# One load of a streamed key cache cut into six, a ring of buffers at another address, and sixteen idle matmuls

## The chip, the cores and the metric

The kernel runs on one core of one Trainium2 chip. Its time is the device time of one execution in microseconds; the kernel before takes 1294.54 us (median of three runs, 1294.46 to 1294.87). Five engines work beside each other: TensorE (PE, its weight loads shown as PEld), VectorE (DVE), ScalarE (ACT), GpSimd (POOL) and SyncE (SP), which here only issues DMAs. The DMAs of the core run on 16 DMA engines; a queue is the way from one issuing engine to those 16.

## The reference

One decoding step of a transformer layer: grouped-query attention over a cache, plus a token-mixing MLP, both on the same normalised input. All arrays are float32.

```python
x: (8, 1, 512); k_cache, v_cache: (8, 8, 8192, 128)      # 268 MB each
q = (layernorm(x) @ wq)                                  # 32 heads of 128, 4 to a cache head
p = softmax(q @ k^T * 128**-0.5)                         # 8192 keys per head
out = x + (p @ v) @ wo + W2 gelu(W1 layernorm(xn) + b1) + b2
```

Each cache element is read once and used by four query heads. The two caches are 536.9 MB of the 553.7 MB that the kernel reads.

## The kernel before, in words

The work runs in 32 steps (`N_PR`). Step `i` takes one batch element and two cache heads: 2 x 8192 keys of 128 numbers, 8 MB of keys and 8 MB of values, laid over 128 partitions with 64 KB in each. One load of a step, keys or values, is a single DMA of 128 rows of 64 KB (`load_next`, L109), issued by SP. The first and last steps use halves of 4 MB (L111).

All loads land in one ring of five slots, `raw`, each of 32 KB in a partition (`slots`, L48). Keys of neighbouring steps lie in slots 0 and 1 or 1 and 2, in turn; values lie in slots 3 and 4. So one slot of the keys of step `i+1` is one that keys of step `i` used, and their load is issued when the first half of the keys of step `i` is scored. The ring stands behind a small tile, `pad` (L46), which holds three weight columns of the MLP and a one-hot table: 74 float32 in a partition, 296 bytes. In the built program, the ring starts at byte 16832 of a partition.

Order is written by hand: `manual_schedule` keeps each engine's instructions as they are coded. In a step, for each half of the keys, DVE turns four blocks in place (L251, four transposes of 2.27 us), and TensorE scores each block (L261); then the row maximum, the exponential, the spread of the probabilities, and TensorE's product with the values of the step before (L302). SP issues the next keys after the first half (`score_half`) and the next values after the product. In the last step the two halves of `wo` follow in the same ring, the second half cut into pieces of 8, 4, 2, 1 and 1 sixteenths of it (L123), so that the closing matmuls (L432, L438) begin before all is there. The output leaves by one DMA of 4 x 8 rows of 512 bytes (L446).

At the start x and b2 are loaded by ACT's queue, the columns for `pad` by POOL's, and `wq` and the first keys by SP's. DVE builds tables (`ident` comes from POOL; `rep`, `hmask`, `send` and others from DVE), TensorE projects the queries (L221, L232) when `wq` is there.

## Time and profile before

| what | value |
|---|---|
| median of three runs | 1294.54 us (1294.46 to 1294.87) |
| the profiled execution: its time, and the span of its instructions | 1294.56 us, 1292.8 us |
| mean granted TensorE clock | 0.808 |
| busy share of the span: PE, DVE, ACT, POOL | 58%, 52%, 16%, 17% |
| DMA: bytes, mean rate | 554.39 MB, 429 GB/s |

The span runs from the first to the last instruction of the program; 1.76 us of the profiled execution's time lie outside it. Shares are means over the whole span. A DMA share of 1.00 in a window means that all 16 DMA engines had a packet under way all the time; a packet is counted in the window in which it starts, so that the share of a short window can be over 1.

### The profile page before, as it was taken

Reading aid. Unit: us, or ns where it says so; the run is one execution under the profiler, and the core shown is the slowest. Engines: PE = TensorE matmul, PEld = TensorE weight load, DVE = VectorE, ACT = ScalarE, POOL = GpSimd, SP = SyncE. Lnnn points to the kernel's source line nnn. Section 1 sums busy time; section 2 is a strip of 40 time slices with the busy share of each in tenths; the row PEclk is TensorE's granted clock in tenths of the full one; section 3 lists DMA queues with packets and bytes.
Section 4 is the critical chain, followed back from the end, with each engine's and each line's share of the span. In section 5 each row is a group of like instructions: output and inputs, shape, how many; then the busy total and the mean of one; then the engine's idle time right before and its main releaser. Section 6 shows DMA issues by size and latency. Waiting matters only on the chain.

```text
span 1292.8 us, 10743 instructions
## 1 busy us (share of the span) xinstructions
PE 751.4 (58%) x4630; PEld 162.6 (13%) x4630; DVE 677.8 (52%) x509; ACT 206.9 (16%) x311; POOL 225.9 (17%) x241
## 2 busy tenths in 40 slices
PE   4366456666556665465575656575455765455566
PEld 1011011111011111011110111111011110011112
DVE  3656654455644465654365644466644565544460
ACT  0002222121222121122111222112222000000000
POOL 0003323131332122233113322212332000000000
PEclk9688777887677897787987877887777887778888
DMA  9999999999999999999999999999999999999997
GB/s 407 428 433 447 424 432 435 432 436 426 439 432 430 430 432 436 432 431 435 430 443 422 435 434 424 443 426 430 442 424 439 430 434 430 428 441 423 434 426 313
DMA packets 11011, 554.39 MB, mean 429 GB/s; under 512 B 1324, under 2 KB 1356, under 8 KB 1748
## 3 DMA queue, kind: packets, MB, share of 16 engines
q1 hardware_dynamic: 10836, 553.67, 99.2%
q8 instruction: 36, 0.59, 0.2%
q14 instruction: 11, 0.09, 0.0%
q0 software_dynamic: 96, 0.02, 0.0%
q10 hardware_dynamic: 32, 0.02, 0.0%
HBM read 553.69 MB, written 0.02 MB: 428 GB/s over the span
## 4 chain that ended last, share of the span: by engine, by line
DMA 73%; DVE 22%; PE 4%; issue 0%; SPq 0%; DVEq 0%
DMA raw<-in_A_k_cache_dram 69%; DVE raw L251 22%; PE acc L261 3%; DMA raw<-in_A_wo_dram 3%; DMA raw<-in_A_wq_dram 2%; PE misc L221 0%; PE acc L302 0%; SPq L123 0%; DVEq L251 0%; PE hb L438 0%; SPq L80 0%; PE misc L279 0%; DVE macc L445 0%; DVEq L445 0%
## 5 line engine op out<-in xcount | busy, mean ns | idle before, releaser
L251 DVE STREAM_TRANSPOSE raw<-raw 128x2048 f32<-128x2048 f32 x256 | 565.4, 2274 | 250.4 <-DMA raw<-in_A_k_cache_dram 250.4
L261 PE MATMUL acc<-raw,z 128*32 128x512 f32 x2048 | 371.3, 810 | 486.9 <-DVE raw L251 474.3
L302 PE MATMUL acc<-raw,pt 128*32 128x512 f32 x2048 | 243.2, 617 | 16.1 <-DMA raw<-in_A_v_cache_dram 15.9
L348 POOL TENSOR_SCALAR g<-g,pad 128x512 f32<-128x512 f32 x112 | 77.4, 691 | 577.7 <-ACT g L347 577.7
L261 PEld LDWEIGHTS acc<-raw,z 128*32 128x32 f32 x2048 | 47.1, 123 | 798.4 <-DVE raw L251 492.8
L349 POOL TENSOR_TENSOR macc<-macc,g 128x512 f32<-128x512 f32 x112 | 141.8, 1266 | 9.3
L287 ACT ACTIVATE t2k<-acc,nb 128x512 f32<-128x512 f32 x32 | 22.0, 687 | 651.9 <-DVE nb L281 651.9
L294 DVE STREAM_TRANSPOSE pt<-misc 128x512 f32<-128x512 f32 x64 | 45.9, 717 | 141.0 <-PE misc L293 136.6
L347 ACT ACTIVATE g<-hb,pad 128x512 f32<-128x512 f32 x112 | 87.0, 777 | 192.4 <-POOL macc L349 191.0
L302 PEld LDWEIGHTS acc<-raw,pt 128*32 128x32 f32 x2048 | 67.2, 113 | 174.5 <-issue 138.7
L281 DVE CUSTOM_DVE_ANT_0 t2k<-misc,hmask 128x128 f32<-128x128 f32 x32 | 9.3, 292 | 121.5 <-PE misc L279 121.5
L293 PE MATMUL misc<-t2k,send 128*128 128x512 f32 x128 | 65.0, 631 | 2.7 <-ACT t2k L287 2.7
L274 DVE TENSOR_REDUCE mr<-acc 128x1 f32<-128x512 f32 x32 | 22.1, 691 | 46.1 <-PE acc L261 46.1
L310 ACT COPY ob<-acc 128x512 f32<-128x512 f32 x32 | 18.7, 585 | 121.6 <-PE misc L326 55.1
L341 POOL MEMSET macc<- 128x512 f32 x8 | 4.2, 526 | 185.0 <-PE misc L353 154.4
L347 ACT ACT_TABLE_LOAD x24 | 30.8, 1283 | 17.9 <-PE hb L339 17.6
L416 ACT ACT_TABLE_LOAD x24 | 30.8, 1283 | 0.4
L326 PE MATMUL misc<-ob,pick 128*32 128x512 f32 (+2 forms) x72 | 29.0, 545 | 0.7 <-ACT ob L310 0.7
L293 PEld LDWEIGHTS misc<-t2k,send 128*128 128x128 f32 x128 | 22.2, 193 | 44.7 <-issue 41.8
L221 PE MATMUL misc<-raw,ob 128*32 128x512 f32 x64 | 10.9, 843 | 12.3 <-DVE mv L145 8.4
L328 DVE TENSOR_TENSOR t2k<-misc,keep 32x512 f32<-32x512 f32 (+2 forms) x9 | 5.7, 629 | 22.6 <-PE misc L326 22.6
L279 PE MATMUL misc<-ident,mr 128*128 128x128 f32 x32 | 10.3, 323 | 0.0
(74 smaller groups left out, 119.6 us busy)
## 6 DMA issues: line engine op xcount, KB each, us to landing
raw<-in_A_v_cache_dram SPq DMA_DIRECT2D x4, 4096.0 KB, 36.3
raw<-in_A_wq_dram SPq DMA_DIRECT2D x2, 4096.0 KB, 17.2
raw<-in_A_k_cache_dram SPq DMA_DIRECT2D x2, 4096.0 KB, 31.0
raw<-in_A_wo_dram SPq DMA_DIRECT2D x1, 4096.0 KB, 29.0
raw<-in_A_wo_dram SPq DMA_DIRECT2D x1, 2048.0 KB
raw<-in_A_wo_dram SPq DMA_DIRECT2D x1, 1024.0 KB, 32.5
raw<-in_A_wo_dram SPq DMA_DIRECT2D x1, 512.0 KB
raw<-in_A_wo_dram SPq DMA_DIRECT2D x2, 256.0 KB, 32.5
```

What stands on the lines that cost most here:

```text
L251: nc.vector.transpose(t, t)
L261: nc.tensor.matmul(SD[i][c * W:(c + 1) * W, :].rearrange("p (t j) -> p t j", j=W), Z[:, q, b, (1 - k) * REP:(1 - k) * REP + W], t[:, c * C ...
L274: nc.vector.tensor_reduce(mr, SD[i], AX.X, ALU.max)
L287: nc.scalar.activation(p, SD.pop(i), AF.Exp, bias=nb, scale=SCALE, accum_out=LD[e][:, o:o + 1])
L293: nc.tensor.matmul(m, send[:, k, :], p, start=True, stop=True)
L294: nc.vector.transpose(PT[k][:, :CH_T * W], m)
L302: nc.tensor.matmul(OD[i][j * W:(j + 1) * W, :].rearrange("p (c d) -> p c d", c=NCH), PT[k][:, t * W:(t + 1) * W], v[:, t], start=(not k an ...
L326: nc.tensor.matmul(mv, pick[:, c, :], ob[:, :n, c * DH:(c + 1) * DH], start=(c == 0), stop=(c == NCH - 1))
L347: nc.scalar.activation(g, hb, AF.Gelu_apprx_tanh, bias=b1t[:, j:j + 1], scale=w1t[:, j:j + 1])
L348: nc.gpsimd.tensor_scalar(g, g, w2t[:, j:j + 1], 1.0, op0=ALU.mult, op1=ALU.mult)
L349: nc.gpsimd.tensor_add(acc, acc, g)
L416: nc.scalar.activation(small.tile([P, 1], F32, name="warm"), nil, AF.Exp)
```

## The change

Three edits stand in one diff.

- `pad` is 96 float32 wide (384 bytes) and no longer 74. In the built program, the ring then starts at byte 16896 of a partition, which is 33 x 512, and no longer at 16832.
- The load of the keys of step 14 is six DMAs and no longer one: the first 24 KB of all 128 rows; then the other 40 KB of rows 0 to 111; then the 40 KB of rows 112 to 116, of 117 to 121, of 122 to 126, and of row 127. All bytes and their places in the ring are the same.
- Sixteen matmuls of 32 columns into a PSUM tile that nothing reads stand ahead of the projection of the queries.

```diff
+PAD = 96
+SHIFT = 16
+TILT = 14
+TILT_P = 112
+TILT_N = 5
+TILT_AT = 6144
...
-    pad = place.tile([P, 3 * NF + W], F32, name="pad")
+    pad = place.tile([P, PAD], F32, name="pad")
...
         rows = rows[:, part[0] * size:(part[-1] + 1) * size]
-        if x is None:
+        if x is None and to is KP and i == TILT:
+            nc.sync.dma_start(t[:, :TILT_AT], rows[:, :TILT_AT])
+            nc.sync.dma_start(t[:TILT_P, TILT_AT:], rows[:TILT_P, TILT_AT:])
+            p = TILT_P
+            while p < P:
+                n = min(TILT_N, P - p)
+                nc.sync.dma_start(t[p:p + n, TILT_AT:], rows[p:p + n, TILT_AT:])
+                p += n
+        elif x is None:
             nc.sync.dma_start(t, rows)
...
+    idle = misc()
+    for j in range(SHIFT):
+        nc.tensor.matmul(idle[j % NB * W:(j % NB + 1) * W, :W], ident[:, :W], rep[:, 0, :W], start=True, stop=True)
```

On SP's queue, around the keys of step 14 (values of step 12, keys of 13, ... before; sizes are rows x float32), the order before has one row for each load:

```order
L109 DMA raw<-in_A_v_cache_dram 128x16384
L109 DMA raw<-in_A_k_cache_dram 128x16384
L109 DMA raw<-in_A_v_cache_dram 128x16384
L109 DMA raw<-in_A_k_cache_dram 128x16384
L109 DMA raw<-in_A_v_cache_dram 128x16384
```

and the changed one has these between the values of step 12 and of step 13:

```order
L123 DMA raw<-in_A_v_cache_dram 128x16384
L115 DMA raw<-in_A_k_cache_dram 128x6144
L116 DMA raw<-in_A_k_cache_dram 112x10240
L120 DMA raw<-in_A_k_cache_dram 5x10240 x3
L120 DMA raw<-in_A_k_cache_dram 1x10240
L123 DMA raw<-in_A_v_cache_dram 128x16384
L123 DMA raw<-in_A_k_cache_dram 128x16384
```

SP has five more instructions to issue there, and nothing else on its queue has changed places.

On TensorE, the program's start before (four transposes of the normalised x, then the projection):

```order
L158 MATMUL misc<-ident,ob 128x8 x4
L221 MATMUL misc<-raw,ob 32x512 x32
L232 MATMUL misc<-ident,t2k 128x32 x8
L240 MATMUL misc<-qt,rep 64x32 x8
L261 MATMUL acc<-raw,z 32x512 x48
```

and now:

```order
L172 MATMUL misc<-ident,ob 128x8 x4
L232 MATMUL misc<-rep,ident 32x32 x16
L239 MATMUL misc<-raw,ob 32x512 x32
L250 MATMUL misc<-ident,t2k 128x32 x8
L258 MATMUL misc<-qt,rep 64x32 x8
L279 MATMUL acc<-raw,z 32x512 x48
```

The sixteen stand between the transposes and the projection; each counts on PE as a weight load and a matmul, so every later instruction of PE has 32 more ahead of it.

## The prediction

> **What bounds the kernel now.** I read the page first: DMA slices, queues, chain.

> ```profile
> DMA  9999999999999999999999999999999999999997
> GB/s 407 428 433 447 424 432 435 432 436 426 439 432 430 430 432 436 432 431 435 430 443 422 435 434 424 443 426 430 442 424 439 430 434 430 428 441 423 434 426 313
> ...
> q1 hardware_dynamic: 10836, 553.67, 99.2%
> q8 instruction: 36, 0.59, 0.2%
> ...
> HBM read 553.69 MB, written 0.02 MB: 428 GB/s over the span
> ```

> SP's queue keeps the 16 DMA engines busy for 99.2% of the span; no compute engine is over 58%. The chain of waits names key loads (69%) and turns of keys (22%), but that is one loop of fixed length: a load, 8.9 us of turning, 1.1 us of scores, the next issue.

> ```profile
> 540.08 27.84 DMA raw<-in_A_k_cache_dram
> ...
> 578.01 28.60 DMA raw<-in_A_k_cache_dram
> 606.61 0.03 issue
> 606.64 0.02 DVEq L251
> 606.66 0.04 issue
> 606.70 8.90 DVE raw L251 x4
> 615.61 0.04 issue
> 615.65 1.11 PE acc L261 x8
> 616.76 0.02 issue
> 616.77 29.85 DMA raw<-in_A_k_cache_dram
> ```

> From issue to landing the load at 578.01 takes 28.60 us. The next window shows 434 GB/s with all engines busy, so 8.39 MB alone take 19.33 us: the load lay 9.3 us in the queue behind the values. Compute may be later by some microseconds before any engine runs dry. What is scarce is the time of the DMA engines. Whether they share it evenly shows only at the end, in windows of 1 us (columns: window, its length, busy time and instructions of PE, PEld, DVE, ACT, POOL, then clock, DMA share, GB/s):

> ```profile
> 200.00:300.00 100.00, 59.69 (x349) 12.57 (x341) 49.16 (x38) 23.28 (x32) 27.92 (x29) 0.80 1.00 434
> ...
> 1280.00:1281.00 1.00, 1.00 (x12) 0.33 (x8) 0.00 (x0) 0.00 (x0) 0.00 (x0) 0.70 0.94 379
> 1281.00:1282.00 1.00, 1.00 (x8) 0.27 (x4) 0.00 (x0) 0.00 (x0) 0.00 (x0) 0.50 0.81 332
> 1282.00:1283.00 1.00, 1.00 (x12) 0.38 (x8) 0.00 (x0) 0.00 (x0) 0.00 (x0) 0.50 0.63 250
> 1283.00:1284.00 1.00, 1.00 (x12) 0.28 (x8) 0.00 (x0) 0.00 (x0) 0.00 (x0) 0.59 0.54 213
> 1284.00:1285.00 1.00, 1.00 (x12) 0.32 (x9) 0.00 (x0) 0.00 (x0) 0.00 (x0) 1.00 0.53 215
> 1285.00:1286.00 1.00, 1.00 (x12) 0.16 (x4) 0.00 (x0) 0.00 (x0) 0.00 (x0) 1.00 0.50 201
> 1286.00:1287.00 1.00, 0.74 (x12) 0.16 (x8) 0.00 (x0) 0.00 (x0) 0.00 (x0) 1.00 0.46 180
> 1287.00:1288.00 1.00, 0.80 (x20) 0.34 (x16) 0.00 (x0) 0.47 (x1) 0.00 (x0) 1.00 0.25 94
> 1288.00:1289.00 1.00, 0.85 (x32) 0.45 (x25) 0.00 (x0) 0.12 (x1) 0.00 (x0) 1.00 0.07 27
> ```

> Between 1281 and 1284 half of the engines run out of work; the other half (share 0.50 to 0.54) goes on until 1287, four of them (0.25) until after 1288. All were given the same bytes. The shares from 1280 on add up to 4.73 us, so 16 engines ending together would end at 1284.7, some 4 us before the last. That is all that a better division can give.

> Where half of them lost time shows in the queue named instruction: 36 packets of 16 KB, the last here:

> ```profile
> q1 hardware_dynamic: 5, 0.04, 44.5%
> q8 instruction: 1, 0.02, 33.4%
> ```

> In this window, 1282.7 to 1282.9, it takes 33.4% of 16 x 0.2 us, 1.07 us of one engine. Single packet records, which no view groups, follow each other on one engine within 3 to 4 ns, so engines can be told apart: PE's 36 fetches go to eight engines in turn, four or five on each, and each puts its engine back by about 1.5 us; ends then differ by up to 7.3 us. The other eight are behind the earliest by 0.0, 0.0, 0.2, 0.3, 0.4, 0.9, 1.9 and 4.3 us.

> **The change part by part.**

> *The six loads.* 434 GB/s over 16 engines is 27.1 GB/s each, so a row of 40 KB takes 1.51 us. Before, each engine has eight such rows. What a load of few rows does is seen in x's eight rows of 2 KB (a window of 0.17 us at 1.69) and in the output's 4 x 8 rows (1291 to 1292):

> ```profile
> q10 hardware_dynamic: 16, 0.02, 27.1%
> ...
> DMA packets 36, 0.02 MB, mean 16 GB/s; under 512 B 4, under 2 KB 36, under 8 KB 36
> q1 hardware_dynamic: 36, 0.02, 5.7%
> ```

> Eight data packets and eight 4-byte ones, which tell of an engine's end: eight engines with a row each. The output's outermost count is four and it has four 4-byte packets: four engines. So 112 rows should be seven on each of 16 engines, five rows one on each of five engines, and a single row one on one. With the same five each time, one engine gets 7+4 rows (+4.53 us), four get 7+3 (+3.02 us), and eleven get 7 (-1.51 us). That holds for the late ones if the five are none of them. Then the last landing moves from 1288.92 (chain below) to 1287.41. The five must not become last: an engine that ended by 1281.6 ends by 1286.1 with 4.53 more, one that ended by 1283.0 ends at 1286.0 with 3.02 more. I take -1.51; bounds +3.02 (a late engine among the five) and -1.51.

> [...]

> What SP pays: five more issues, 0.33 us each by the next row, 1.7 us. Behind them stands the load of the values of step 13, issued some 16 us after the keys of step 14, so this costs nothing. The six land together 1 us or so later than the one did (4.5 to 5.0 us behind the earliest engine instead of 3.6, by the records), and turns, scores and the issue at 578.01 follow; the 9.3 us in the queue covers it. Without that cover it would cost the same 1 us.

> ```profile
> L109 SPq DMA_DIRECT2D raw<-in_A_k_cache_dram x31: 327/328/333, 28.4 to 1201.7; - x31
> ```

> *The tail* has to pass the gain on.

> ```profile
> 1279.09 7.05 PE L432 MATMUL acc<-raw,ot 128*32 128x512 f32 x48 [2.58 <-DMA raw<-in_A_wo_dram]
> 1286.40 1.06 PE L432 MATMUL acc<-raw,ot 128*32 128x512 f32 x8 [0.26 <-DMA raw<-in_A_wo_dram]
> 1288.97 0.43 PE L438 MATMUL hb<-raw,ot 128*32 128x128 f32 x8 [0.15 <-DMA raw<-in_A_wo_dram]
> ...
> 1256.30 32.62 DMA raw<-in_A_wo_dram
> ```

> Its start at 1279.09, its resumption at 1286.40 and its last product at 1288.97 all wait for landings, and all of these are the late engines'. They move together; 3.88 us from 1288.92 to the span's end stay.

> *The ring's address.* Ten packets of 64 KB (44 to 46 us):

> ```profile
> q1 hardware_dynamic: 10, 0.66, 75.7%
> ```

> 75.7% of 32 engine-microseconds is 2.42 us for each. The output's 36 packets take 5.7% of 16 us, 0.91 us; at 27.1 GB/s its 16 KB are 0.60 us of that, so each packet has about 8.5 ns beside its bytes. An engine has 10836/16 = 677 packets; an address can save at most 677 x 8.5 ns = 5.8 us, at least nothing. Those 8.5 ns are met also where no long row is written, which speaks for the lower end: I take -0.3.

> *Sixteen idle matmuls.*

> ```profile
> 13.58 5.54 PE L221 MATMUL misc<-raw,ob 128*32 128x512 f32 x32 [8.44 <-DVE mv L145]
> 41.91 1.07 PE L240 MATMUL misc<-qt,rep 128*64 128x32 f32 x16 [11.66 <-DVE qt L233]
> ```

> The nearest row is sixteen matmuls of 32 columns in 1.07 us. They lie in the 8.44 us in which PE waits ahead of the projection: 0; without that wait 1.07. They also move each fetch 32 instructions ahead, some 4 us in mid-kernel. A fetch moved stays on its engine: 0, bounds -1.07 and +1.07.

> *Sum:* span 1292.8 - 1.51 - 0.3 = 1291.0; with the 1.76 us outside the span 1292.75. The profiled execution (1294.56) stands 0.02 above the median: **1292.7 us**. A difference of 0.2% (2.6 us) is about what a measurement of this kernel can tell from no change.

> **The rivals.**

> *The address saves more.* If the start of each packet loses 2 to 4 of its 8.5 ns, 677 packets give 1.4 to 2.7 us beside the 1.51: 1290.3 to 1291.6. For it: every packet into the ring is concerned. Against: the same 8.5 ns on small packets elsewhere.

> *One of the five is 4.3 us late already.* With 3.02 more it ends about where the last one ends now: no gain, 1294.2. The first five have to be drawn badly for this; nothing in a view names them.

> *The five rows meet late engines* (slower). One that bears PE's fetches and gets 3.02 us more is last: 1288.92 + 3.02, less 0.3, gives 1297.3. It decides as soon as an engine that now ends after 1285.9 is among the five. [...]

> *Neighbouring partitions share one way into SBUF* (slower). If four partitions took no more than one engine's 27.1 GB/s, rows 112 to 115 would take 6.05 us together and not 1.51, and the following ones would crowd likewise: the engine with four extra rows would need up to 15 us for them and not 6, and end at 1295 instead of 1286: about 1300.8. Against it: x's row above. 16 KB went into partitions 0 to 7 within 0.17 us, 48 GB/s for each four. Packets of 2 KB may be buffered, 40 KB hardly, so I keep it.

> [...]

> **How the numbers follow.** Forecast 0.55, of which I count 0.03 as faster by over 0.2%; the address saves more 0.22; no gain 0.10; late engines 0.08; shared way 0.05. Faster by over 0.2% (below 1291.95): 0.25. Slower by over 0.2% (above 1297.1): 0.12, with the part of late engines that ends just below left aside. Within: 0.63. The range: 1290.4 covers the first rival nearly whole, 1295.8 the case of no gain with a microsecond of crowding; beyond lie the two slower rivals with 0.13. The forecast's own range is 1291.9 to 1293.7.

> **What would show it.** Right: the DMA share in 1281 to 1284 stays higher than before, the last landing comes 1.5 us earlier, the tail behind it is unchanged. The ring: ten packets of 64 KB still at 2.42 us; 2.418 or less would be the first rival. The six loads: keys of step 14 land by about 1 us later, and the next issue follows. Wrong: that load takes over 30 us, or the share at the end falls earlier and has a longer thin tail; then one engine carries more than it should.

## The result and the profile after

The changed kernel takes 1313.99 us (median of four runs, 1313.23 to 1314.18) beside 1294.5 us for the kernel before (1294.44 to 1294.87): a ratio of 1.0149, 95% interval 1.0137 to 1.0161. It is slower by 19.5 us. The profiled execution's span is 1312.0 us.

The DMA part of the page of the changed kernel shows where: slices of 32.8 us, in the second row GB/s.

```profile
DMA  9999999999999999999999999999999999999997
GB/s 402 436 441 440 426 436 429 434 440 434 430 432 434 434 432 434 391 207 424 432 434 432 436 430 432 434 434 428 438 436 434 427 436 434 432 434 436 432 426 307
```

One slice falls to 207 GB/s and its neighbour to 391; in the kernel before none but the last was under 407. The row above does not move: the engines count as busy throughout. Cut into windows of 20 us (columns as in the prediction), the place is the load of the keys of step 14:

```profile
520.00:540.00 20.00, 8.61 (x40) 0.98 (x40) 12.19 (x7) 4.02 (x6) 7.82 (x8) 0.57 1.03 443
540.00:560.00 20.00, 16.62 (x107) 4.07 (x104) 8.20 (x9) 0.78 (x2) 0.00 (x0) 0.91 1.02 331
560.00:580.00 20.00, 2.12 (x6) 0.40 (x3) 2.73 (x4) 7.24 (x9) 10.28 (x11) 0.65 1.09 206
580.00:600.00 20.00, 4.91 (x28) 0.88 (x32) 9.05 (x5) 0.00 (x0) 0.00 (x0) 0.58 0.89 313
600.00:620.00 20.00, 15.70 (x109) 3.48 (x108) 10.60 (x9) 2.91 (x5) 0.00 (x0) 0.91 0.99 426
```

Against 434 GB/s the three windows from 540 to 600 miss (103 + 228 + 121) GB/s x 20 us = 9.0 MB, which is 20.8 us at 434. A DMA share of 1.09 beside 206 GB/s means packets that are under way and hardly move. In the chain of waits the six loads show as one wait, whose last piece the view gives to an unknown queue:

```profile
540.10 46.53 DMA raw<-in_A_k_cache_dram
...
586.67 4.06 another core or an unknown queue
...
590.95 8.90 DVE raw L269 x4
599.85 0.04 issue
599.89 1.11 PE acc L279 x8
601.00 0.02 issue
601.02 28.05 DMA raw<-in_A_k_cache_dram
```

DVE begins to turn these keys at 590.95, 52.1 us after the first of the six issues (538.83); in the kernel before it was 27.9 (540.08 to 567.94). The next key load is issued at 601.02 and no longer at 578.01. The load after it takes 28.05 us, as usual.

### The profile page after: what moved, and what is told of

It reads as the page before. It is cut to its first block, busy times and chain, and to the rows that moved or that the text cites. A ratio compares the mean times of both kernels' runs of the same rounds, so it can differ in the third digit from the quotient of the medians.

```text
span 1312.0 us, 10819 instructions
## 1 busy us (share of the span) xinstructions
PE 756.7 (58%) x4662; PEld 162.0 (12%) x4662; DVE 677.8 (52%) x509; ACT 206.9 (16%) x311; POOL 225.9 (17%) x241
## 2 busy tenths in 40 slices
DMA  9999999999999999999999999999999999999997
DMA packets 11171, 554.39 MB, mean 423 GB/s; under 512 B 1356, under 2 KB 1388, under 8 KB 1780
## 3 DMA queue, kind: packets, MB, share of 16 engines
q1 hardware_dynamic: 10996, 553.67, 99.2%
HBM read 553.69 MB, written 0.02 MB: 422 GB/s over the span
## 4 chain that ended last, share of the span: by engine, by line
DMA 73%; DVE 22%; PE 4%; issue 0%; another core or an unknown queue 0%; SPq 0%; DVEq 0%
DMA raw<-in_A_k_cache_dram 69%; DVE raw L269 22%; PE acc L279 3%; DMA raw<-in_A_wo_dram 2%; DMA raw<-in_A_wq_dram 2%; PE misc L239 0%; PE acc L320 0%; SPq L137 0%; DVEq L269 0%; PE hb L456 0%; SPq L116 0%; SPq L86 0%; SPq L120 0%; PE misc L297 0%
## 5 line engine op out<-in xcount | busy, mean ns | idle before, releaser
L279 PE MATMUL acc<-raw,z 128*32 128x512 f32 x2048 | 376.8, 821 | 502.9 <-DVE raw L269 470.3
L365 ACT ACT_TABLE_LOAD x24 | 30.8, 1283 | 17.9 <-PE hb L357 17.6
L434 ACT ACT_TABLE_LOAD x24 | 30.8, 1283 | 0.4
L258 PE MATMUL misc<-qt,rep 128*64 128x32 f32 x64 | 3.0, 243 | 12.8 <-DVE qt L251 12.8
```

The source lines that it names most:

```text
L279: nc.tensor.matmul(SD[i][c * W:(c + 1) * W, :].rearrange("p (t j) -> p t j", j=W), Z[:, q, b, (1 - k) * REP:(1 - k) * REP + W], t[:, c * C ...
L365: nc.scalar.activation(g, hb, AF.Gelu_apprx_tanh, bias=b1t[:, j:j + 1], scale=w1t[:, j:j + 1])
L434: nc.scalar.activation(small.tile([P, 1], F32, name="warm"), nil, AF.Exp)
```

## The experiments

### One part at a time

Changed kernel without the six loads (the ring and the idle matmuls stay):

```diff
-TILT = 14
+TILT = -1
```

> The changed kernel with the keys of step 14 loaded by one DMA again; the ring's new address and the sixteen idle matmuls stay. Its trace against that of before: in 540 to 620 us the changed kernel moved some 21 us less of data than at its full rate, and everywhere else a load of 8 MB took 19.32 us instead of 19.35. Theory A (the six loads cost all of the loss, the address gains): 60 loads x 0.031 us less, 1292.6 us, ratio 0.9985. Theory B (the address or the matmuls cost a part of the loss too): above 1295.

Measured: 1291.63 us beside 1294.58, ratio 0.9978 (0.9969 to 0.9987). All of the loss is in the six loads, and what remains of the change is a gain, of 3.0 us where 1.9 was expected.

Kernel before with the ring alone moved:

```diff
-    pad = place.tile([P, 3 * NF + W], F32, name="pad")
+    pad = place.tile([P, 96], F32, name="pad")
```

> The kernel before with the ring at byte 16896 instead of 16832, nothing else. If the address is what makes packets of 64 KB take 2.418 us instead of 2.420 to 2.427: a load of 8 MB in 19.32 us, 1292.6 us, ratio 0.9985. If the idle matmuls were the cause of the faster packets: 1294.5, ratio 1.000.

Measured: 1291.55 us (1291.31 to 1291.97) beside 1294.58, ratio 0.9977 (0.9968 to 0.9986). It beats both kernels, and it is level with the changed kernel without the six loads, in which the idle matmuls stay: the gain is the ring's.

Kernel before with the idle matmuls alone:

```diff
+    idle = misc()
+    for j in range(16):
+        nc.tensor.matmul(idle[j % NB * W:(j % NB + 1) * W, :W], ident[:, :W], rep[:, 0, :W], start=True, stop=True)
```

> The kernel before with the sixteen idle matmuls alone. They fill an idle stretch of 8.4 us at the start and put PE's fetches 32 instructions ahead. Prediction's step: 1294.5 us, ratio 1.000 (within 0.0008 for a fetch more or less on the last engine). Rival: they cause the faster packets, 1292.6.

Measured: 1294.59 us, ratio 1.0001 (0.9992 to 1.0009). The timeline of TensorE in this kernel shows why (start, length, then the instruction and in brackets the idle time ahead of it):

```profile
6.51 0.66 PE L218 MATMUL misc<-rep,ident 128*32 128x32 f32 x32 [0.89 <-DVE rep L163]
13.69 5.00 PE L225 MATMUL misc<-raw,ob 128*32 128x512 f32 x32 [6.53 <-DMA raw<-in_A_wq_dram]
```

They take 0.66 us and end 6.53 us before `wq` is there.

The six loads alone, with the ring where it was:

```diff
-PAD = 96
-SHIFT = 16
+PAD = 74
+SHIFT = 0
```

> The kernel before with the six loads alone: the ring stays at its old address and there are no idle matmuls. If the parts add up: the six loads cost 1313.99 less 1291.6, 22.4 us, so 1294.5 + 22.4 = 1316.9 us (1315.5 to 1318.0). If the loss hangs on the new address (an aligned ring letting engines meet at the same place), it is much smaller: 1294.5 to 1305 us.

Measured: 1318.37 us, ratio 1.0184 (1.0169 to 1.0199). That is 23.8 us on top of the kernel before, where the six loads on the moved ring cost 1313.99 - 1291.63 = 22.4. The median lies 0.4 us above the range that was given and the interval reaches well into it: the loss does not hang on the new address, and the parts add up to within 1.4 us.

### Which of the six loads

The cut alone: 24 KB and 40 KB, both of all 128 rows.

```diff
-TILT_P = 112
+TILT_P = 128
```

> The changed kernel with its cut at 24 KB but both parts of all 128 rows: two loads, no division among engines changed. Writing-side theory: no packet shares its way, so nothing lost, 1291.6 us as without the cut. If the cut as such (40 KB rows, or starting 24 KB into a row) cost something: above 1293.

Measured: 1291.76 us, ratio 0.9978 (0.9969 to 0.9987). A load cut in two in this way costs nothing that these runs can tell (1291.63 without the cut). Its windows and its chain beside those above:

```profile
540.00:560.00 20.00, 17.38 (x109) 4.29 (x105) 8.37 (x9) 0.78 (x2) 0.00 (x0) 0.91 0.95 410
560.00:580.00 20.00, 10.31 (x44) 1.28 (x42) 15.97 (x11) 7.24 (x9) 10.33 (x11) 0.66 1.01 434
```

```profile
538.54 28.13 DMA raw<-in_A_k_cache_dram
...
577.71 27.53 DMA raw<-in_A_k_cache_dram
```

Then the 40 KB of 112 rows, and one load of 16 rows in place of four:

```diff
-TILT_N = 5
+TILT_N = 16
```

> The changed kernel with the last sixteen rows in one load of 16 rows instead of 5, 5, 5 and 1. The 112 rows stay as they are. By the probe, 32 KB rows: 112 rows took 14.9 us from the first packet to the last and 128 rows 10.9; sixteen neighbouring rows 4.7 and one row 1.2 or so. Writing-side theory: most of the 22.4 us stays, since the 112 rows and what runs beside them stay crowded; the sixteen rows at once crowd their four groups for about 6 us of 40 KB rows, instead of some 15 us for the chain of four behind each other, so between 1300 and 1312. If the few rows on five engines alone were the loss: 1292 to 1294.

Measured: 1311.06 us (1309.76 to 1311.45), ratio 1.0125 (1.0110 to 1.0140). 19.4 of the 22.4 us are still there. The form 5, 5, 5, 1 is worth the other 3.

And a cut at 120 rows, which I took for harmless:

```diff
-TILT_P = 112
-TILT_N = 5
+TILT_P = 120
+TILT_N = 8
```

> The changed kernel, but the keys of step 14 in three loads: 24 KB of all 128 rows, 40 KB of rows 0 to 119, and 40 KB of rows 120 to 127. The ring and the idle matmuls stay. Theory that a load loses time where its engines' runs of rows no longer lie in the partitions that each engine has alone in a load of 128 rows: 120 rows are eight on each of 15 engines, so each engine stays in its own partitions, the 120 rows run at the full rate, and only the last eight rows crowd, four to a way: by the probe (four neighbouring rows of 32 KB in 4.3 us) 5.4 us for 40 KB where one row alone takes 1.5. Eight engines end at most 4 us later and one gets 12 us less: 1292 to 1296 us, beside 1311 for the cut at 112 rows with one load of 16 behind it. Rival, that any cut into fewer than 128 rows costs what the cut at 112 did: 1305 to 1313 us. If the 120 rows go not to 15 engines but to 8 with 15 rows each, 11 us or more on top of 1291.6 come from that alone; the packets would show it.

Measured: 1315.24 us (1312.81 to 1317.14), ratio 1.0153 (1.0136 to 1.0170). My expectation of 1292 to 1296 is refuted, and the median lies above the rival's 1305 to 1313 too. The packets of 4 bytes on SP's queue, of which a load of 128 rows has sixteen (80 in 1100 to 1200 us of the kernel before, beside five such loads), are 1227 here and 1204 in the kernel with one load: 23 more, as they are if the 120 rows went to 15 engines and the eight rows to eight (16 + 15 + 8 less 16). If a load of 128 rows and one of 120 both gave each engine eight neighbouring rows, those 120 rows would have been expected to lose nothing; so at least one of the two seems to be divided in another way, and no run shows which. The theory of ways itself, with four partitions and the four 32 further on, had said otherwise for 120 rows, had I applied it: if engine i carries rows 8i to 8i+7, its first four rows and those of engine i+4 lie on one way. That was put to a test of its own, the last one below.

The packet records (no view groups them by size; sums over all packets of a size on SP's queue, divided by 16, in us per engine) show what grew:

```
                          24 KB    40 KB     64 KB
cut at 128 rows            7.30    12.11   1161.94
112 + 16 rows              8.36    25.61   1166.45
112 + 5 + 5 + 5 + 1 rows   8.44    25.28   1168.84
120 + 8 rows               8.68    27.50   1167.40
```

All rows have the same number of packets of each size. In the changed kernel the 40 KB packets take 13.2 us longer per engine, the 64 KB packets 6.9 and the 24 KB packets 1.1: 21.2 of the 22.4 us by which the spans of the first and third row differ (1289.6 and 1312.0). The 64 KB packets belong to the load queued beside it, the values of step 13: up to 7.7 us for a packet of 2.418. That load has all 128 rows, and 6.3 of its 6.9 us are in packets that start between 569.5 and 589.5 us; the last 40 KB packet ends at 589.7. That they are slow because the 40 KB rows write into their ways is the theory; the times agree with it.

### What a load of few rows costs by itself

Three probes put loads of rows of 32 KB (or less, where it says so) into slot 4 ahead of the kernel with the ring alone moved. Where two loads touch the same partitions, the second is issued when the first has landed; the times of these kernels as wholes say nothing. Each probe ran once. In the code `p4` is slot 4, `N4` is 32 KB in float32, and the rows of `far` lie 64 KB apart in the cache, those of `near` 32 KB. The lines, here of the first:

```diff
...
+    nc.sync.dma_start(p4, far[:P, :N4])
+    nc.sync.dma_start(p4[:112], far[:112, :N4])
+    nc.sync.dma_start(p4[:112], near[:112])
+    nc.sync.dma_start(p4, far[:7 * P:7, :N4])
...
+    nc.sync.dma_start(p4[:64], far[:64, :N4])
+    nc.sync.dma_start(p4[::2], far[:64, :N4])
+    nc.sync.dma_start(p4[:16], far[:16, :N4])
...
+    nc.sync.dma_start(p4[:4], far[:4, :N4])
+    nc.sync.dma_start(p4[:16:4], far[:4, :N4])
+    nc.sync.dma_start(p4[:5], far[:5, :N4])
...
```

> Fourteen loads of 32 KB rows into one slot ahead of all others, each waiting for the one before, so that each is seen alone; the result is not touched, the time is some 80 us longer and not of interest. Theory A1 (writing side: each group of four neighbouring partitions, shared with the group 32 further on, takes only one engine's 27.1 GB/s): from issue to landing, 2 us or so beside: 128 rows 9.7 us; 112 rows over 9.7, from sources at either distance; 64 neighbouring rows 9.7, 64 alternate rows 4.8 to 6; 16 neighbouring rows 4.8, 16 rows four or eight apart 2.4; 4 neighbouring rows 4.8, 4 rows four apart 1.2; five rows 4.8; one row 1.2. Theory A2 (reading side: which rows of the cache are read together decides): 112 rows from rows 32 KB apart unlike 112 rows from rows 64 KB apart, 128 rows from rows 448 KB apart slow, and 4, 5 and 16 rows 1.2 us however they lie in SBUF.

Its timeline of SP's queue (start of the issue, its length, line). The distance from one row to the next is the time of one load with its latency:

```profile
0.74 0.39 SPq L80 DMA_DIRECT2D raw<-in_A_k_cache_dram  x1
13.38 0.35 SPq L81 DMA_DIRECT2D raw<-in_A_k_cache_dram  x1
29.74 0.32 SPq L82 DMA_DIRECT2D raw<-in_A_k_cache_dram  x1
46.05 0.35 SPq L83 DMA_DIRECT2D raw<-in_A_k_cache_dram  x1
58.06 0.35 SPq L84 DMA_DIRECT2D raw<-in_A_k_cache_dram  x1
70.21 0.58 SPq L85 DMA_DIRECT2D raw<-in_A_k_cache_dram  x1
82.94 0.50 SPq L86 DMA_DIRECT2D raw<-in_A_k_cache_dram  x1
90.48 0.34 SPq L87 DMA_DIRECT2D raw<-in_A_k_cache_dram  x1
...
107.11 0.32 SPq L90 DMA_DIRECT2D raw<-in_A_k_cache_dram  x1
113.51 0.66 SPq L91 DMA_DIRECT2D raw<-in_A_k_cache_dram  x1
117.34 0.26 SPq L92 DMA_DIRECT2D raw<-in_A_k_cache_dram  x1
```

128 rows take 12.64 us, 112 rows 16.36: fewer bytes, more time. The source does not matter: 112 rows from places half as far apart take 16.31, and 128 rows from places seven times as far apart 12.01, so the reading side falls. The destination does: 64 neighbouring rows take 12.73 us (L85), 64 alternate ones 7.54 (L86). Four neighbouring rows take 6.40 (L90), four rows four apart 3.83 (L91). By the packet records the four neighbouring rows take 4.26 us from first start to last end, 131 KB, 30.8 GB/s for the four partitions together, next to the 27.1 GB/s of one engine. The rows apart were expected in 1.2 us and took 2.08 by the packet records: the first packets of a load are longer (up to 2.2 us in the load of 128 rows, where the median is 1.213), so the ratio is two and not four.

Alone, the 112 rows lose 4.0 us to the 128 (14.9 and 10.9 by the packet records). The 22.4 us in the kernel, where other loads are queued beside them, are not worked out from these times.

The second probe varies the size of four neighbouring rows and of four rows four apart (2, 4, 8, 16, 32 KB, in pairs), then takes eight neighbouring rows of 2 and of 32 KB and two rows at distance 1, 32 and 64:

```diff
...
+    nc.sync.dma_start(p4[:4, :512], far[:4, :512])
+    nc.sync.dma_start(p4[:16:4, :512], far[:4, :512])
...
+    nc.sync.dma_start(p4[:2], far[:2, :NT * DH])
+    nc.sync.dma_start(p4[:64:32], far[:2, :NT * DH])
+    nc.sync.dma_start(p4[:128:64], far[:2, :NT * DH])
...
```

> Sixteen loads of few rows ahead of all others, each alone, with rows of 2, 4, 8, 16 and 32 KB; the time is not of interest. The prediction took x's eight rows of 2 KB in 0.17 us for a sign that neighbouring partitions do not share one way in. If the shared way is hidden by what small packets have in flight: four neighbouring rows of 2 KB as fast as four rows four apart (first packet to last end under 0.2 us), and from 8 or 16 KB on up to four times slower. If it is not size that hides it: neighbours slower by the same factor at every size. Two rows 32 apart as slow as two neighbours, two rows 64 apart as fast as one row, if the group is shared with the one 32 further on.

In SP's timeline, 2 KB neighbouring and four apart stand first, 16 KB (L84, L85), 32 KB (L86, L87), and the pairs of rows (L90 to L92) behind:

```profile
0.74 0.38 SPq L78 DMA_DIRECT2D raw<-in_A_k_cache_dram  x1
2.54 0.73 SPq L79 DMA_DIRECT2D raw<-in_A_k_cache_dram  x1
4.72 0.26 SPq L80 DMA_DIRECT2D raw<-in_A_k_cache_dram  x1
...
13.53 0.26 SPq L84 DMA_DIRECT2D raw<-in_A_k_cache_dram  x1
17.32 0.60 SPq L85 DMA_DIRECT2D raw<-in_A_k_cache_dram  x1
20.20 0.26 SPq L86 DMA_DIRECT2D raw<-in_A_k_cache_dram  x1
26.23 0.60 SPq L87 DMA_DIRECT2D raw<-in_A_k_cache_dram  x1
30.25 0.28 SPq L88 DMA_DIRECT2D raw<-in_A_k_cache_dram  x1
...
38.26 0.23 SPq L90 DMA_DIRECT2D raw<-in_A_k_cache_dram  x1
42.50 0.54 SPq L91 DMA_DIRECT2D raw<-in_A_k_cache_dram  x1
47.35 0.48 SPq L92 DMA_DIRECT2D raw<-in_A_k_cache_dram  x1
51.05 0.23 SPq L93 DMA_DIRECT2D raw<-in_A_k_cache_dram  x1
```

Rows of 2 KB show nothing: neighbouring 1.80 us, four apart 2.18. At 16 KB the neighbours land 0.9 us later (3.79 and 2.88), though by the packet records both loads' packets are over after 1.19 and 1.17 us. So at 16 KB the packets' ends do not show what the landings show. At 32 KB the packets show it too: 4.10 and 2.26 us, landings 6.03 and 4.02, which is less than the factor of four that was expected. So x's rows of 2 KB, on which the prediction leaned, could not tell neighbouring partitions from others. Two rows at distance 1 take 4.24 us, at 32 take 4.85, at 64 take 3.70 (2.41, 2.61 and 2.08 by the packet records): 32 apart is no quicker than neighbouring, as the theory has it for one shared way, and 64 apart is quicker by 0.54 us.

The third probe tests the theory on counts and places not tried before:

```diff
...
+    nc.sync.dma_start(p4, far[:P, :N4])
+    nc.sync.dma_start(p4[:120], far[:120, :N4])
+    nc.sync.dma_start(p4[16:], far[:112, :N4])
+    nc.sync.dma_start(p4[:96], far[:96, :N4])
+    nc.sync.dma_start(p4[64:], far[:64, :N4])
...
+    nc.sync.dma_start(p4[:32], far[:32, :N4])
+    nc.sync.dma_start(p4[:128:32], far[:4, :N4])
...
```

> A probe: ahead of the kernel with the ring alone moved, thirteen loads of rows of 32 KB into slot 4, each waiting until the one before has landed; the result is untouched. In order: 128 rows; 120 rows; 112 rows at the upper end; 96 rows; 64 neighbouring rows at the upper end; 64 alternate odd rows; 32 rows four apart; 32 neighbouring rows; four rows 32 apart; four rows two apart; the last eight rows; 128 rows again; one row. Each takes from its issue to the next about 1.5 us more than its data. Theory of ways: a way into SBUF takes one engine's rate and serves partitions 4g to 4g+3 and the same 32 further on; in a load of 128 rows each engine has just one way, in a load of another count engines meet at ways. Data times expected: 128 rows 10.9 us; 120 rows 17 to 20 (two engines on one way for most of it); 112 rows about 15 as at the lower end; 96 rows 12 to 15; 64 upper neighbouring rows 10.6 and 64 odd alternate ones 5.9, as their counterparts; 32 rows four apart 2.5 to 3.5, 32 neighbouring ones 4.9 to 6; four rows 32 apart 2.4 to 2.7 (two on each of two ways); four rows two apart 2.4 to 2.7; the last eight rows 4.3. Rival, that what costs is the number of rows alone, with each engine at home in eight neighbouring partitions: 120 rows 10.9 to 11.5, 32 rows alike in both places, four rows 32 apart 1.3.

```profile
0.74 0.40 SPq L80 DMA_DIRECT2D raw<-in_A_k_cache_dram  x1
13.39 0.42 SPq L81 DMA_DIRECT2D raw<-in_A_k_cache_dram  x1
35.50 0.32 SPq L82 DMA_DIRECT2D raw<-in_A_k_cache_dram  x1
52.72 0.31 SPq L83 DMA_DIRECT2D raw<-in_A_k_cache_dram  x1
69.33 0.58 SPq L84 DMA_DIRECT2D raw<-in_A_k_cache_dram  x1
81.95 0.50 SPq L85 DMA_DIRECT2D raw<-in_A_k_cache_dram  x1
```

With their latency 128 rows take 12.65 us, 120 rows 22.11, 112 rows at the upper end 17.22, 96 rows 16.61 and 64 neighbouring ones 12.62. From first packet to last the 120 rows take 20.5 us where the theory of ways said 17 to 20 and its rival 10.9 to 11.5; 112, 96 and 64 rows take 15.5, 14.8 and 10.6, within or a little past their ranges (that of the 112 rows was taken from the first probe). 32 neighbouring rows take 5.5, four rows 32 apart 2.59, where the rival said 1.3 and two rows 64 apart had taken 2.08. The 64 odd rows and the 32 rows four apart were issued together, since they share no partition, and so were the four rows two apart and the last eight; these four are not told apart. The first two, 96 rows, took 8.3 us together with a median packet of 1.213 us, that of the first probe's 128 rows, where 96 neighbouring rows took 14.8: the place costs, and not the number.

Which engine carries which row, no run here shows, and by the theory no one division explains all loads: eight neighbouring rows on each engine would give the time of the 120 rows (two engines on each way, 16 packets of 1.21 us or 19.4 us, and the start), but four rows of the list on each would make the engines of the 64 alternate rows meet likewise, and those and the 32 rows four apart ran at a median of 1.213 us a packet. That the loss follows from the partitions written is shown (8.3 and 14.8 us for 96 rows); that engines meet, and which, stays open.

### The ring's address

Two more places, multiples of 128 (byte 17024) and of 256 (byte 17152) and of no higher power of two:

```diff
-    pad = place.tile([P, 3 * NF + W], F32, name="pad")
+    pad = place.tile([P, 128], F32, name="pad")
```

> The kernel before with the ring at byte 17024 of a partition, a multiple of 128 and not of 256. Which multiple counts: if 128 is enough, 1291.6; if not, 1294.5. The packets' own times tell it beside: a load of 8 MB in 19.32 or in 19.35 us.

Measured: 1294.39 us, ratio 0.9999 (0.9989 to 1.0008).

```diff
-    pad = place.tile([P, 3 * NF + W], F32, name="pad")
+    pad = place.tile([P, 160], F32, name="pad")
```

> The kernel before, with the ring moved to byte 17152 of each partition: a multiple of 256 and of no greater power of two (before: 16832, a multiple of 64; the change: 16896, a multiple of 512). Nothing else differs. The move to a multiple of 512 alone gave 1291.55 us beside 1294.58, and the move to 17024, a multiple of 128, gave 1294.39 beside 1294.5, no gain. Theory that a write into SBUF is cut at 512 bytes: 256 gives at most half of the gain, 1293 to 1294.6 us. Theory that it is cut at 256 bytes: the whole gain, 1291.3 to 1292.0 us. The profile would show it in the time of a 64 KB packet: 2.418 us with the gain, 2.420 without.

Measured: 1291.56 us, ratio 0.9977 (0.9967 to 0.9986), the whole gain. Of the four places, those at a multiple of 512 and of 256 gain (1291.55 and 1291.56 us), those at 64 and 128 do not (1294.59 and 1294.39). The prediction's window of 44 to 46 us, now of the kernel with the ring alone moved, has six packets:

```profile
q1 hardware_dynamic: 6, 0.39, 45.3%
```

45.3% of 32 engine-microseconds is 2.416 us each, where ten took 2.42 before. The single records are finer: 2.418 us in 7645 of 7808 packets, and a mean of 2.4211; before, a mean of 2.4249 and times from 2.418 to 2.427 in 7571 packets; at the multiple of 128 a mean of 2.4250, at that of 256 one of 2.4218. 3.8 ns on 488 packets of 64 KB per engine is 1.84 us; all packets of the queue together are 2.16 us shorter (1282.52 and 1280.36 us per engine). The chain of the moved ring ends

```profile
1253.46 32.48 DMA raw<-in_A_wo_dram
```

at 1285.94, which is 2.98 before the 1288.92 of the kernel before. The other 0.8 us is not resolved; how the late engines fall may be in it.

## Why the prediction was wrong

**What bounds the kernel** was read rightly: the time of the DMA engines. The bytes that were not moved are, at the rate of before, 20.8 of the 22.4 us.

**The six loads** are the step that failed: "434 GB/s over 16 engines is 27.1 GB/s each, so a row of 40 KB takes 1.51 us", and from it -1.51 us with bounds of +3.02 and -1.51. The division of rows agrees with the counts: the changed kernel has 32 packets of 4 bytes more than the one before (1356 and 1324 under 512 bytes on the pages), as many as 16 + 16 + 5 + 5 + 5 + 1 less 16. That the same five engines take every load of five rows, from which the prediction adds up its +4.53, +3.02 and -1.51, was an assumption of mine: no run shows which engines they were, and in place of these sums the runs showed a cost of 22.4 us. The price of a row did not: a 40 KB packet took 25.28/8 = 3.16 us on the mean. I priced rows by the engine that carries them and left out where they are written. A row cost 1.51 us in every packet of the cut at 128 rows, and between 2.06 and 5.72 us in the changed kernel; that engines meet at the ways there is the theory. The term was +22.4 us, outside both bounds, because both came from the same price.

**The landing** "1 us or so later", hidden by 9.3 us in the queue, came some 23 us later: the next issue moved from 577.71 (cut at 128 rows) to 601.02. The cover was real and far too small. The prediction's own sign of being wrong, a load of over 30 us, was there.

**The tail** was to pass on a gain that a better division makes. None is to be seen. In the changed kernel the windows of 1 us at the end read (the DMA share stands last but one)

```profile
1301.00:1302.00 1.00, 0.95 (x12) 0.04 (x3) 0.00 (x0) 0.00 (x0) 0.00 (x0) 1.00 0.77 313
...
1303.00:1304.00 1.00, 0.92 (x12) 0.32 (x16) 0.00 (x0) 0.00 (x0) 0.00 (x0) 1.00 0.48 188
1304.00:1305.00 1.00, 1.00 (x12) 0.09 (x4) 0.00 (x0) 0.00 (x0) 0.00 (x0) 1.00 0.13 53
...
1307.00:1308.00 1.00, 0.95 (x32) 0.52 (x24) 0.00 (x0) 0.25 (x1) 0.00 (x0) 1.00 0.04 16
```

What is missing to 1.00 in the seven windows from 1301 to 1308 adds up to 4.7 us. In the kernel with the ring alone moved it is 3.9 us in eight windows, of which these are the first and the last:

```profile
1278.00:1279.00 1.00, 1.00 (x8) 0.27 (x4) 0.00 (x0) 0.00 (x0) 0.00 (x0) 0.50 0.82 338
...
1285.00:1286.00 1.00, 0.95 (x34) 0.52 (x26) 0.00 (x0) 0.24 (x1) 0.00 (x0) 1.00 0.11 41
```

Half of the engines no longer trail by 4 us, but one or two (shares of 0.13 to 0.04 from 1304 on) go on for 4 us behind the rest.

**The ring's address**: that an address can shorten the packets held, and so did the bounds (0 to -5.8); the size did not: -0.3 was taken, -3.0 measured. The first rival, 2 to 4 ns of each packet, has the size that was found, 3.8 ns on the mean of a packet of 64 KB, and packets of 2.418 us were its sign; that the time is lost at a packet's start, no run shows. The argument against it, that small packets elsewhere show the same 8.5 ns, could not separate a cost of the address from a cost of every packet.

**The idle matmuls**: 0, as said (1294.59 us beside 1294.58). On the pages they are 32 matmuls and 32 weight loads (4662 of each after, 4630 before), 64 instructions of PE where the section on the change and the prediction count 32. **SP's five issues** were not run by themselves; beside the 21.2 us of the packets, 1.2 us is left for them and all else.

**The rivals.** The shared way, at a chance of 0.05, is the one that the probes speak for (four neighbouring rows of 32 KB take 4.26 us, four rows four apart 2.08), and its price was too small as well: 1300.8, since it counted only the last 16 rows. The 112 rows and the load beside them are likely to carry most of the loss (the run with one load of 16 rows keeps 19.4 us), but no run has the 112 rows without the last sixteen behind them. It was put low on the word of x's row, and the second probe shows that rows of 2 KB are as quick in neighbouring partitions as four apart (1.80 and 2.18 us).

The parts measured each by itself add up to 1294.5 - 3.0 + 23.8 = 1315.3 us, 1.3 above the changed kernel's 1313.99, with runs of the loads alone between 1317.11 and 1319.84.

## What to carry to other kernels

The load of 128 partitions here was not 16 equal shares that could be cut anywhere: with rows of 32 KB, 128 rows took 12.65 us and 120 rows 22.11. Try first to keep loads of long rows at 128 rows (cutting the rows' length, at 24 KB, cost nothing here: 1291.76 and 1291.63 us), and price any other count by where its rows are written (64 neighbouring rows took 12.73 us, 64 alternate ones 7.54). When the busy share stays at 9 and GB/s falls, as in the slice of 207 GB/s here, look at the time of single packets: here those of 40 KB took 3.16 us on the mean where 1.51 was the time without the loss. Try the start of a large buffer at a multiple of 256 bytes in the partition, which gave 0.23% here (byte 16832 moved to 16896 or to 17152).

## What the runs showed of the hardware that was not expected

- 120 rows take longer than 128 (20.5 us and 11.0 us for rows of 32 KB), and so do 112 (14.9) and 96 (14.8).
- 64 alternate rows land in 7.5 us, 64 neighbouring ones in 12.7.
- Four neighbouring rows of 16 KB end their packets in 1.19 us, as quickly as four rows four apart (1.17), and land 0.9 us later.
- With the ring's start at a multiple of 512 bytes a packet of 64 KB takes 3.8 ns less on the mean than at 64 (2.4211 and 2.4249 us); the place at a multiple of 256 gives the same time of the kernel (1291.56 and 1291.55 us), the one at a multiple of 128 saves nothing (1294.39).
